# A two-layer attention and GLU kernel on one core: key copies and wo splits on GpSimd, weight squares and query products ahead of the first scores

## The chip, the cores and the metric

The kernel runs on one core of a Trainium2 chip. A core has a matrix engine (TensorE, PE in the profile, its weight loads PEld), a vector engine (VectorE, DVE), an activation engine (ScalarE, ACT), GpSimd (POOL) and an engine that mostly issues transfers (SyncE, SP). Each works through its own list of instructions in order. The metric is device time in microseconds, as the median of several runs.

## The reference

Two layers of the same weights; each is attention and a gated linear unit, both with a residual.

```python
def _A_ref(x, wq, wk, wv, wo):
    q = (x @ wq).reshape(B, S, H, Dh).transpose(0, 2, 1, 3)
    k = x @ wk
    v = x @ wv
    scores = jnp.einsum("bhqd,bkd->bhqk", q, k) * (Dh ** -0.5)
    p = _softmax(scores, axis=-1)
    o = jnp.einsum("bhqk,bkd->bhqd", p, v)
    return o.transpose(0, 2, 1, 3).reshape(B, S, H * Dh) @ wo

def _B_ref(x, w_gate, w_up, w_down):
    g = jnp.einsum("bsd,df->bsf", x, w_gate)
    u = jnp.einsum("bsd,df->bsf", x, w_up)
    return jnp.einsum("bsf,fd->bsd", _sigmoid(g) * u, w_down)

x = x + _A_ref(_layernorm(x), ...);  x = x + _B_ref(_layernorm(x), ...)   # twice
```

S is 2048, D 448, F 1792; 16 heads of 28 share one set of keys and values. The transposes are written shorter here than in the source.

## The kernel before

**Numbers.** Products of 32-bit values are made from 16-bit halves: each operand is split into a high part and a remainder, and one product is a chain of eleven matmuls (line 363). A weight is scaled by a power of two first, which is found from the sum of its squares: `squares` (L109) on ScalarE, `scales` on VectorE. `wo` is split on the way in by `split_d` (ScalarE the high part, VectorE the remainder, L130 and L131) and `split_p` (ScalarE, then GpSimd in two operations, L135 to L137), in turn.

**First stage.** The loop over `i` takes sixteen tiles of 128 rows of x through normalisation, the high/low split `hl` (remainder on GpSimd, L333 and L334), transposes (t, then XT on ScalarE, L348), the product with the key and value weights (kv), and `build()`: ScalarE writes the key's high part `ktl` and the value VV, VectorE the key's remainder (L394), and a copy (L396) repeats the high part six times. An iteration later `kvt` (L402, L403) transposes that into keys, and ScalarE copies them to KK (L406). Every four tiles GpSimd finds the group's reciprocal deviation in eight small operations (L317 to L325).

**Query products.** `qp` are chains at L363; ScalarE evicts each one to `qst` (L420) and, ahead of the main loop, to `qf` (L423) as well; GpSimd makes the remainder (L428), and a transfer that it issues (L435) stores both to `qd`, from which SP's queue loads QS.

**Maxima.** Before a query block's scores, each row's maximum over the keys has to be known. `Maxima.step()` makes four products `mx` (L556) and four reductions on VectorE (L561); a query block of 512 takes sixteen steps. After the last, `row_max` (L572) reduces, transposes (`mt`), copies (`mr`), and GpSimd issues the transfer of `mr` into QS (L585). `first_mx` calls the steps of query block 0 from the first stage: from iteration `SM` on one in each iteration, then the rest.

**Main loop.** A step is one query block u and one key tile kt. In the order `FSFSFSFSPXM` it issues fillers F (pieces of query products, later of the GLU), four score products s (L591) with an exponential on ScalarE each (P, L594), the previous step's pv (L602), and a maxima step of the next query block. The steps listed in `MORE` make two maxima steps. All but pv share seven banks of PSUM.

**Weights of the GLU.** `prep_b` is a generator: wo's load, its squares, its split, then 24 pieces (8 of each of three weights, 128x784, L194) whose squares are summed, then splits of columns and rows. `PLAN` gives how many of its steps have been taken by a step of the main loop, and `first_mx` takes some ahead of it. Pieces lie in the two buffers of tag XT2.

The lines that decide the order around the change:

```python
SM = L4 + 3 + 1
...
    if i >= SM:
        first_mx()
        nmx += 1
```

Of the kernel before, what the change touches and what calls it, by code (L numbers as in the profile page):

```python
# [8 lines left out]
F32 = mybir.dt.float32  # L9
# [10 lines left out]
def interleaved_layers_kernel(ctx: ExitStack, tc: tile.TileContext, x, wq, wk, wv, wo, wg, wu, wd, out, layers=2):  # L20
# [6 lines left out]
    nc = tc.nc  # L27
    _, S, D = x.shape
# [154 lines left out]

    def prep_b():

        NPG = 8
        mall = wk1.tile([128, 3, NPG], F32, name="mall", bufs=1)
        FL = D * F // 128 // NPG
        todo, raw = [], []

        def piece(w, i):
            wf = w.rearrange("a b -> (a b)").rearrange("(p n) -> p n", p=128)
            r = wk1.tile([128, FL], F32, tag="XT2", name="rmax")
            nc.sync.dma_start(r, wf[:, i * FL:(i + 1) * FL])  # L194
            return r

        def columns(f):
            r = big.tile([128, 2, 4, 128], F32, tag="big", name="rgu")
            for j, w in enumerate((wg, wu)):
                load4(r[:, j], w[:, f * 128:(f + 1) * 128])  # L200
            return r

        def rows(f):
            r = big.tile([128, 2, D], F32, tag="big", name="rd")
            nc.sync.dma_start(r, wd[f * 128:(f + 2) * 128].rearrange("(j p) n -> p j n", p=128))
            return r

        def get():

            while todo and len(raw) < 2:  # L210
                fn, *args = todo.pop(0)
                raw.append(fn(*args))
            return raw.pop(0)


        ro = [wk1.tile([128, 2, D], F32, tag="x1", name="ro") for _ in range(2)]
        for c in range(2):
            nc.gpsimd.memset(ro[c], 0.0)
            for g in range(G):
                nc.sync.dma_start(ro[c][32 * g:32 * g + Dh],  # L220
                                  wo[(4 * g + 2 * c) * Dh:(4 * g + 2 * c + 2) * Dh].rearrange("(h d) n -> d h n", d=Dh))
        yield
        parts = wk1.tile([128, 2], F32, name="parto", bufs=1)
        for c in range(2):
            junk = wk1.tile([128, 2, D], F32, tag="XT2", name="juno")
            squares(parts[:, c:c + 1], ro[c], junk)
        yield
        nc.vector.tensor_reduce(mxb[:, 0:1], parts, axis=AX.X, op=OP.add)
        yield
        yield from scales(mxb[:, 0:1], 1, pwb[:, 0:1], swb[:, 0:1])  # L230
        nc.vector.tensor_scalar(osc, pwb[:, 0:1], pwa[:, 1:2], 2.0 ** -23, op0=OP.mult, op1=OP.mult)
        for c in range(4):
            (split_d, split_p)[c % 2](WO[:, 0, c], WO[:, 1, c], ro[c // 2][:, c % 2], swb[:, 0:1])
            if c == 2:
                todo += [(piece, w, i) for w in (wg, wu, wd) for i in range(NPG)]
                for _ in range(2):
                    fn, *args = todo.pop(0)
                    raw.append(fn(*args))
            yield
        ready[0] = 1  # L240


        for n in range(3 * NPG):
            r = raw.pop(0) if raw else get()
            squares(mall[:, n // NPG, n % NPG:n % NPG + 1], r, r)
            while todo and len(raw) < 2:
                fn, *args = todo.pop(0)
                raw.append(fn(*args))
            yield
        todo += [(columns, f) for f in range(FC)] + [(rows, f) for f in range(0, FC, 2)]  # L250
        raw.append(columns(todo.pop(0)[1]))
        nc.vector.tensor_reduce(mxb[:, 1:4], mall, axis=AX.X, op=OP.add)
        yield
        yield from scales(mxb[:, 1:4], 3, pwb[:, 1:4], swb[:, 1:4])
        nc.vector.tensor_scalar(gsc, pwb[:, 1:2], 2.0 ** -26, None, op0=OP.mult)
        nc.vector.tensor_scalar(dsc, pwb[:, 2:3], pwb[:, 3:4], 2.0 ** -23, op0=OP.mult, op1=OP.mult)
        for f in range(FC):
            r = get()
            st = big.tile([128, 2, 2, 4, 128], F16, tag="big", name="sgu")
            for j in (1, 0):  # L260
                (split_d, split_pp)[j](st[:, j, 0], st[:, j, 1], r[:, j], swb[:, 1 + j:2 + j])
                if j == 0:
                    def store(f=f, st=st):
                        nc.gpsimd.dma_start(wgu_d[f].rearrange("p j l c n -> p (j l c n)"),
                                            st.rearrange("p j l c n -> p (j l c n)"))
                        ready[0] += 1
                    defer(store, 3)
                yield
        for f in range(0, FC, 2):
            r = get()  # L270
            for j in range(2):
                (split_d, split_pp)[1 - j](WD[:, f + j, 0], WD[:, f + j, 1], r[:, j], swb[:, 3:4])
            yield
        ready[0] += 1
        yield


    PLAN = [(0, 8), (28, 32), (31, 35), (63, 63), (71, 70)]
    prepd = [0]

    def paced(step):
# [100 lines left out]
    def kv(l, XT, t, kt, start=False):  # L382

        p = fps([128, 56], F32, "kv")
        yield from chain(p, lambda a, c, k: WKV[:k, a, c], lambda c, k: XT[:k, c, t * 128:(t + 1) * 128], 40, False)
        kt_ = ktl[kt % 2]

        def build():
            if start:
                nc.scalar.activation(kt_[:, 0, 0:28], p[:, 0:28], AF.Copy, scale=2.0 ** -18)  # L390
            else:
                nc.vector.tensor_scalar(kt_[:, 0, 0:28], p[:, 0:28], 2.0 ** -18, None, op0=OP.mult)
            nc.scalar.activation(VV[l][:, kt, 0:28], p[:, 28:56], AF.Copy, scale=2.0 ** -16)
            nc.vector.scalar_tensor_tensor(kt_[:, 1, 0:28], p[:, 0:28], 2.0 ** -18, kt_[:, 0, 0:28],  # L394
                                           op0=OP.mult, op1=OP.subtract)
            nc.vector.tensor_copy(kt_[:, 2:8, 0:28], kt_[:, 0:1, 0:28].to_broadcast([128, 6, 28]))  # L396
        defer(build)

    def kvt(l, kt, ev=nc.vector.tensor_copy):
# [563 lines left out]
    pkv, pq = prep_kv(), prep_q()  # L963
    nmx, nst, LEAD = 0, 0, 2
    SQ = L2 + 3 + 1
    SM = L4 + 3 + 1
    A0 = 0.5
    PRE, POST = {7: 2}, {6: 1, 8: 1, 9: 2, 10: 2}

    def first_mx():  # L970

        while QDONE.get((0, 0), 0) <= nmx % G and QDONE.get((0, 0), 0) < G:
            fill.slice(QCH / 2)
        if nmx == 0 or 3 < nmx < 12:
            next(prep[0])
            prepd[0] += 1
        mxs[0].step()

    for i in range(NT + L4):
# [30 lines left out]
    while nmx < 4 * NB:  # L1010
        fill.slice(A0E * QCH)
        first_mx()
        nmx += 1

    early[0] = False
    ORDER = "FSFSFSFSPXM"
    MORE = (5, 10)
    HEAD = (U * KT - 32, U * KT - 28, U * KT - 16)
    FIRST = KT * TB + 17
    KEEP = 28000  # L1020
# [1 line left out]
    for l in range(layers):  # L1022
# [3 lines left out]
            late.pop(0)[1]()  # L1026
        if not l:
            mx.step()
        if not final:
            layer_tiles(l + 1)  # L1030
        if l:
            for b in range(2, NB):
                fill.add(qgen(l, b), G * QCH)
        flush(True)
        fill.slice(0.75 * QCH)
        prevP = None
        rate = 0.0
        for step in range(U * KT):
# [91 lines left out]
```

## Time and profile before

| what | us |
|---|---|
| median of the runs (2326.1 to 2327.1) | 2326.68 |
| the profiled execution | 2324.3 |
| its span | 2321.3 |
| start of the first exponentials of the main loop | 93.69 |
| start of those of step 32 (query block 2) | 205.26 |
| start of those of step 52 | 277.33 |

The span is one execution's, from its first to its last instruction; some 3 us of the execution lie around it. A row of a timeline reads: start, duration, engine, line and operation, tile written and tile read, their shapes, how many stand in the row, and in brackets the idle time ahead of it with what ended it. A row of windows gives each engine's busy time in a stretch, then the clock granted to TensorE as a share of the full one, the share of the DMA engines' time, and GB/s.

### The profile page before, as it was taken

Reading aid. Unit: us, or ns where it says so; the run is one execution under the profiler, and the core shown is the slowest. Engines: PE = TensorE matmul, PEld = TensorE weight load, DVE = VectorE, ACT = ScalarE, POOL = GpSimd, SP = SyncE. Lnnn points to the kernel's source line nnn. Section 1 sums busy time; section 2 is a strip of 40 time slices with the busy share of each in tenths; the row PEclk is TensorE's granted clock in tenths of the full one; section 3 lists DMA queues with packets and bytes.
Section 4 is the critical chain, followed back from the end, with each engine's and each line's share of the span. In section 5 each row is a group of like instructions: output and inputs, shape, how many; then the busy total and the mean of one; then the engine's idle time right before and its main releaser. Section 6 shows DMA issues by size and latency. Waiting matters only on the chain.

```text
span 2321.3 us, 41368 instructions
## 1 busy us (share of the span) xinstructions
PE 2225.1 (96%) x15786; PEld 1004.9 (43%) x15786; DVE 1638.1 (71%) x2908; ACT 1585.8 (68%) x2614; POOL 339.4 (15%) x606
## 2 busy tenths in 40 slices
PE   5898899999999999999999999999999999999999
PEld 3222244444444444444563224444444444444456
DVE  6888887777777777777884557767677777767322
ACT  6698777677767777776515887767676767767731
POOL 6204762100110110101002010000000000000010
PEclk9799999999999999999999999999999999999999
DMA  4244671423313132332341113223231313223233
GB/s 118 68 118 126 203 223 41 107 76 95 101 61 108 44 110 73 95 98 76 106 132 40 30 54 100 78 83 98 72 87 57 107 47 105 68 83 95 76 101 114
DMA packets 205639, 213.28 MB, mean 92 GB/s; under 512 B 137520, under 2 KB 165872, under 8 KB 205440
## 3 DMA queue, kind: packets, MB, share of 16 engines
q1 hardware_dynamic: 200064, 195.77, 28.9%
q0 software_dynamic: 5376, 14.87, 1.9%
q8 instruction: 123, 2.02, 0.4%
q14 instruction: 76, 0.62, 0.1%
HBM read 175.37 MB, written 23.59 MB: 86 GB/s over the span
## 4 chain that ended last, share of the span: by engine, by line
PE 57%; DVE 3%; DMA 1%; ACT 1%; issue 1%; SPq 0%; POOL 0%; DVEq 0%; POOLq 0%; ACTq 0%
PE pv L602 13%; PE s L591 12%; PE dn L791 8%; PE up L363 8%; PE gp L363 8%; PE mx L556 4%; DVE mp L561 2%; PE wo L702 2%; PE qp L363 1%; ACT P L594 1%; DMA wgu<-wgu_d 1%; SPq L459 0%; DVE oT L683 0%; DVE th L761 0%; DMA XT<-hl 0%
## 5 line engine op out<-in xcount | busy, mean ns | idle before, releaser
L594 ACT ACTIVATE P<-s,esc 128x512 f32<-128x512 f32 x2048 | 1323.8, 689 | 460.4 <-PE s L591 434.0
L561 DVE TENSOR_REDUCE mp<-mx 128x1 f32<-128x512 f32 x2048 | 1269.8, 683 | 422.0 <-PE mx L556 419.7
L591 PE MATMUL s<-QS,KK 96*128 96x512 f16 x2048 | 767.6, 383 | 42.4 <-DVE mp L561 20.8
L363 PEld LDWEIGHTS <-wgu 128*128 128x128 f16 x4928 | 457.9, 97 | 239.0 <-issue 95.9
L602 PE MATMUL pv<-P,VV 128*32 128x512 f32 x4096 | 548.8, 608 | 0.0
L363 PE MATMUL gp<-XT,wgu 128*128 128x256 f16 x2464 | 375.0, 273 | 0.0
L363 PE MATMUL up<-XT,wgu 128*128 128x256 f16 x2464 | 373.9, 273 | 0.5 <-ACT P L594 0.4
L791 PE MATMUL dn<-WD,h 128*128 128x448 f16 x1344 | 321.0, 353 | 0.0
L591 PEld LDWEIGHTS <-KK 96*128 96x128 f16 x2048 | 197.5, 97 | 155.6 <-issue 60.4
L556 PE MATMUL mx<-KK,QH 32*128 32x512 f16 (+1 forms) x2080 | 222.3, 386 | 10.0 <-ACT P L594 4.0
L556 PEld LDWEIGHTS <-QH 32*128 32x128 f16 x2080 | 53.9, 91 | 393.1 <-issue 390.6
L791 PEld LDWEIGHTS <-h 128*128 128x128 f16 x1344 | 124.1, 98 | 137.7 <-issue 25.5
L602 PEld LDWEIGHTS pv<-P,VV 128*32 128x32 f32 x4096 | 81.1, 108 | 200.4 <-issue 198.0
L764 ACT ACTIVATE h<-th 128x512 f16<-128x512 f32 x112 | 70.3, 628 | 108.5 <-DVE th L761 108.3
L676 POOL TENSOR_TENSOR lb<-pvs,lb 128x512 f32<-128x512 f32 x32 | 40.9, 1278 | 608.3 <-DMA lb<-sums 517.1
L317 POOL TENSOR_SCALAR rs<-mv 128x1 f32<-128x1 f32 (+2 forms) x52 | 12.2, 234 | 797.1 <-DVE mv L302 757.1
L363 PE MATMUL qp<-XT,WQ 128*128 128x512 f16 x352 | 117.7, 400 | 1.9 <-DVE mp L561 0.7
L765 DVE SCALAR_TENSOR_TENSOR h<-th,h 128x512 f16<-128x512 f32 x112 | 78.9, 704 | 34.5 <-ACT h L764 34.5
L753 ACT ACTIVATE th<-gp,gsc 128x512 f32<-128x512 f32 x112 | 76.6, 684 | 38.5 <-PE gp L363 38.4
L761 DVE SCALAR_TENSOR_TENSOR th<-th,up 128x512 f32<-128x512 f32 x112 | 76.1, 680 | 37.3 <-PE up L363 30.9
L702 PE MATMUL wo<-WO,oT 128*128 128x448 f16 x384 | 94.7, 358 | 4.4 <-ACT oT L682 4.3
L363 PEld LDWEIGHTS <-WQ 128*128 128x128 f16 x352 | 34.1, 100 | 67.2 <-issue 43.5
(134 smaller groups left out, 847.2 us busy)
## 6 DMA issues: line engine op xcount, KB each, us to landing
wgu<-wgu_d SPq DMA_DIRECT2D x224, 512.0 KB
QS<-qd SPq DMA_DIRECT2D x384, 32.0 KB
lb<-sums SPq DMA_DIRECT2D x128, 64.0 KB
xr<-in_A_x_dram SPq DMA_DIRECT2D x32, 224.0 KB
qd<-qst POOLq DMA_DIRECT2D x28, 256.0 KB, 2.6
wgu_d<-sgu POOLq DMA_DIRECT2D x14, 512.0 KB, 3.8
QH<-qd SPq DMA_DIRECT2D x28, 128.0 KB
x2d<-x SPq DMA_DIRECT2D x16, 224.0 KB
```

The lines of the kernel that those rows point to most:

```text
L363: nc.tensor.matmul(ps, a, b, start=n == 0, stop=n == 10)
L556: nc.tensor.matmul(ps[h][:, i * w:(i + 1) * w], qh[32 * h:32 * h + 32, g], KK[l][32 * h:32 * h + 32, 1, ka:kz], start=True, stop=True, til ...
L561: nc.vector.tensor_reduce(o, ps[h].rearrange("p (g k) -> p g k", g=n), axis=AX.X, op=OP.max)
L591: nc.tensor.matmul(s, KK[l][0:96, 0, kt * 128:(kt + 1) * 128], QS[l, u][:, g].rearrange("p h n -> p (h n)"), start=True, stop=True)
L594: nc.scalar.activation(p, s, AF.Exp, scale=esc)
L602: nc.tensor.matmul(v[32 * g:32 * g + 32], VV[l][:, kt], P[g], start=kt == 0, stop=kt == KT - 1, tile_position=(0, 32 * g))
L702: nc.tensor.matmul(p, v["oT"][:, a, h * 128:(h + 1) * 128], WO[:, c, h], start=n == 0, stop=n == 11)
L753: defer(lambda: nc.scalar.activation(th, gp.rearrange("p j n -> p (j n)"), AF.Tanh, scale=gsc))
L761: nc.vector.scalar_tensor_tensor(t, th, 1.0, up.rearrange("p j n -> p (j n)"), op0=OP.add, op1=OP.mult)
L764: nc.scalar.activation(h[:, 0], t, AF.Copy, scale=2.0 ** -17)
L765: defer(lambda: nc.vector.scalar_tensor_tensor(h[:, 1], t, 2.0 ** -17, h[:, 0], op0=OP.mult, op1=OP.subtract), 1)
L791: nc.tensor.matmul(p, hs[f // 2][:, a, o:o + 128], WD[:, f, c], start=n == 0, stop=n == 3 * FC - 1)
```

## The change

GpSimd makes the copy of the key's parts in layer 0 from the fourth key tile on, and the remainder of all four parts of wo. The first maxima step comes an iteration earlier. The weights of the GLU are squared in 21 pieces of 128x896, whose buffers are three of tag `wgu` and two of XT2, so that up to five are on their way; 14 of the 21 come ahead of the first scores, with two evictions of query products between and behind them. Ten more query products and one more maxima step are issued ahead of the first scores, and step 5 of the main loop makes one maxima step instead of two.

```diff
-        NPG = 8
+        NPG = 7
...
-        def piece(w, i):
+        def piece(w, i, k):
...
-            r = wk1.tile([128, FL], F32, tag="XT2", name="rmax")
+            if k % 5 < 3:
+                r = wk1.tile([128, FL], F32, tag="wgu", name="rmax", bufs=WB)
+            else:
+                r = wk1.tile([128, FL], F32, tag="XT2", name="rmax")
...
-        def get():
-
-            while todo and len(raw) < 2:
+        def fetch(n):
+            while todo and len(raw) < n:
                 fn, *args = todo.pop(0)
                 raw.append(fn(*args))
+
+        def get():
+            fetch(2)
             return raw.pop(0)
...
+        todo += [(piece, w, i, NPG * j + i) for j, w in enumerate((wg, wu, wd)) for i in range(NPG)]
+        fetch(3)
         yield
...
         for c in range(4):
-            (split_d, split_p)[c % 2](WO[:, 0, c], WO[:, 1, c], ro[c // 2][:, c % 2], swb[:, 0:1])
...
+            split_p(WO[:, 0, c], WO[:, 1, c], ro[c // 2][:, c % 2], swb[:, 0:1])
+            fetch(5)
             yield
...
         for n in range(3 * NPG):
-            r = raw.pop(0) if raw else get()
+            r = get()
             squares(mall[:, n // NPG, n % NPG:n % NPG + 1], r, r)
...
+            fetch(4)
             yield
...
-    PLAN = [(0, 8), (28, 32), (31, 35), (63, 63), (71, 70)]
+    PLAN = [(0, 23), (24, 30), (31, 32), (63, 60), (71, 67)]
...
-            nc.vector.tensor_copy(kt_[:, 2:8, 0:28], kt_[:, 0:1, 0:28].to_broadcast([128, 6, 28]))
+            eng = nc.gpsimd if l == 0 and kt > 2 else nc.vector
+            eng.tensor_copy(kt_[:, 2:8, 0:28], kt_[:, 0:1, 0:28].to_broadcast([128, 6, 28]))
...
-    SM = L4 + 3 + 1
+    SM = L4 + 3
...
+    def advance(n):
+        for _ in range(n):
+            next(prep[0])
+            prepd[0] += 1
+
     def first_mx():
...
-        if nmx == 0 or 3 < nmx < 12:
-            next(prep[0])
-            prepd[0] += 1
+        advance(1 if nmx == 0 or 3 < nmx < 12 else 2 if nmx == 12 else 3 if nmx > 12 else 0)
         mxs[0].step()
...
+    advance(3)
+    fill.slice(1.2 * QCH)
     early[0] = False
     ORDER = "FSFSFSFSPXM"
-    MORE = (5, 10)
+    MORE = (10,)
...
         if not l:
             mx.step()
+            fill.slice(0.4 * QCH)
+            mx.step()
...
-        fill.slice(0.75 * QCH)
+        fill.slice((0.75 if l else 0.4) * QCH)
```

The engines' orders show where things came to stand. First GpSimd, before, in the first stage: `hl` is the remainder of x, `rs` the group's reciprocal deviation, `qst` the remainder of a query product.

```order
L333 TENSOR_TENSOR hl<-xr_153,hl 128x64
L334 TENSOR_TENSOR hl<-xr_153,hl 128x384
L317 TENSOR_SCALAR rs<-mv 128x4
L318 TENSOR_TENSOR rs<-rs,mhalf 128x4
L319 TENSOR_TENSOR rs<-rs 128x4
L320 TENSOR_TENSOR rs<-rs 128x4
L321 TENSOR_SCALAR rs<-rs 128x4
L322 TENSOR_TENSOR rs<-rs 128x4
L324 TENSOR_SCALAR rs<-mv 128x4
L325 TENSOR_TENSOR rs<-rs 128x4
L428 TENSOR_TENSOR qst<-qf,QH_125 128x512
L333 TENSOR_TENSOR hl<-xr_199,hl 128x64
```

The same place in the change:

```order
L398 COPY ktl_111<-ktl_111 128x6x28
L334 TENSOR_TENSOR hl<-xr_153,hl 128x64
L335 TENSOR_TENSOR hl<-xr_153,hl 128x384
L318 TENSOR_SCALAR rs<-mv 128x4
L319 TENSOR_TENSOR rs<-rs,mhalf 128x4
L320 TENSOR_TENSOR rs<-rs 128x4
L321 TENSOR_TENSOR rs<-rs 128x4
L322 TENSOR_SCALAR rs<-rs 128x4
L323 TENSOR_TENSOR rs<-rs 128x4
L325 TENSOR_SCALAR rs<-mv 128x4
L326 TENSOR_TENSOR rs<-rs 128x4
L430 TENSOR_TENSOR qst<-qf,QH_125 128x512
```

Here the next row is the copy of key tile 7, `L398 COPY ktl_112<-ktl_112 128x6x28`: it stands behind the eight operations of `rs` and the remainder of a query product; before, VectorE made it.

Second, GpSimd from the end of the first stage to the transfer of the maxima, before:

```order
L334 TENSOR_TENSOR hl<-xr_382,hl 128x384
L136 TENSOR_SCALAR ro<-ro,swb 128x448
L137 TENSOR_TENSOR WO<-ro,WO 128x448
L136 TENSOR_SCALAR ro<-ro,swb 128x448
L137 TENSOR_TENSOR WO<-ro,WO 128x448
L428 TENSOR_TENSOR qst<-qf,qst 128x512
L435 DMA qd_108<-qst 128x2x512
L585 DMA QS<-mr 1x16x128
```

And in the change, from the second of the four splits of wo on:

```order
L398 COPY ktl_111<-ktl_111 128x6x28
L136 TENSOR_SCALAR ro<-ro,swb 128x448
L137 TENSOR_TENSOR WO<-ro,WO 128x448
L398 COPY ktl_112<-ktl_112 128x6x28
L136 TENSOR_SCALAR ro<-ro,swb 128x448
L137 TENSOR_TENSOR WO<-ro,WO 128x448
L430 TENSOR_TENSOR qst<-qf,qst 128x512
L437 DMA qd_108<-qst 128x2x512
L430 TENSOR_TENSOR qst<-qf,qst 128x512
L437 DMA qd_108<-qst 128x2x512
```

The transfer of the maxima (`L587 DMA QS<-mr 1x16x128`) follows on the last row. Each of the last three copies stands behind a split of wo, and the maxima's transfer behind two remainders and two transfers to `qd` rather than one of each.

Third, ScalarE at the same place, before:

```order
L130 ACTIVATE WO<-ro,swb 128x448
L406 COPY KK<-kvt 128x2x128
L135 ACTIVATE WO<-ro,swb 128x448
L420 ACTIVATE qst<-qp 128x512
L423 ACTIVATE qf<-qp 128x512
L420 ACTIVATE qst<-qp 128x512
L594 ACTIVATE P<-s,esc 128x512 x8
L109 ACTIVATE rmax,mall<-rmax 128x784
```

And in the change:

```order
L135 ACTIVATE WO<-ro,swb 128x448
L408 COPY KK<-kvt 128x2x128
L109 ACTIVATE rmax,mall<-rmax 128x896 x8
L422 ACTIVATE qst<-qp 128x512
L425 ACTIVATE qf<-qp 128x512
L109 ACTIVATE rmax,mall<-rmax 128x896 x6
L422 ACTIVATE qst<-qp 128x512
L425 ACTIVATE qf<-qp 128x512
L422 ACTIVATE qst<-qp 128x512
L596 ACTIVATE P<-s,esc 128x512 x4
L109 ACTIVATE rmax,mall<-rmax 128x896
```

Squares (`rmax`, a piece) stand between the last keys and the two evictions, and in the main loop fewer stand between the exponentials.

More of the change, by code (lines that the diff above doesn't have):

```diff
@@ L232, in prep_b @@
         for c in range(4):
-            (split_d, split_p)[c % 2](WO[:, 0, c], WO[:, 1, c], ro[c // 2][:, c % 2], swb[:, 0:1])
[L234 to L238, printed above, removed]
+            split_p(WO[:, 0, c], WO[:, 1, c], ro[c // 2][:, c % 2], swb[:, 0:1])
+            fetch(5)
             yield
@@ L243, in prep_b @@
         for n in range(3 * NPG):
-            r = raw.pop(0) if raw else get()
+            r = get()
             squares(mall[:, n // NPG, n % NPG:n % NPG + 1], r, r)
-            while todo and len(raw) < 2:
-                fn, *args = todo.pop(0)
-                raw.append(fn(*args))
+            fetch(4)
             yield
```

## The prediction

> **What bounds the kernel now.** The page's busy times come first, because they say where a saved microsecond can count.
>
> ```profile
> PE 2225.1 (96%) x15786; PEld 1004.9 (43%) x15786; DVE 1638.1 (71%) x2908; ACT 1585.8 (68%) x2614; POOL 339.4 (15%) x606
> ```
>
> TensorE is busy for 96% of 2321.3 us. It waits mainly in the beginning, and from step 52 of the main loop on every engine's order is the same in both kernels. So the whole difference has to arise before step 52, and I read only that part: windows of ten microseconds around the last preparation, then the timeline.
>
> ```profile
> core 0: us, PE busy (x) PEld busy (x) DVE busy (x) ACT busy (x) POOL busy (x), PEclk, DMA share, GB/s
> 70.00:80.00 10.00, 8.72 (x40) 2.37 (x40) 10.00 (x21) 2.87 (x8) 4.89 (x4) 0.50 0.00 1
> 80.00:90.00 10.00, 5.75 (x28) 1.52 (x28) 9.24 (x18) 1.08 (x2) 2.30 (x3) 0.84 0.08 26
> 90.00:100.00 10.00, 9.78 (x41) 2.94 (x39) 7.14 (x14) 6.90 (x13) 1.00 (x2) 0.81 0.08 28
> ```
>
> Between 70 and 90 us VectorE is full, ScalarE nearly empty (3.95 of 20 us), and the DMAs carry almost nothing. That is the hole the change works in. The timeline shows what ends it:
>
> ```profile
> 76.33 12.04 DVE L561 TENSOR_REDUCE mp<-mx 128x1 f32<-128x512 f32 x20
> 81.07 0.60 ACT L420 ACTIVATE qst<-qp 128x512 f16<-128x512 f32 x1 [6.15 <-PE qp L363]
> 82.23 1.16 POOL L428 TENSOR_TENSOR qst<-qf,qst 128x512 f16<-128x512 f32 x1 [4.69 <-ACT qf L423]
> 83.69 0.84 POOL L435 DMA_DIRECT2D qd<-qst  x1 [0.30 <-POOL qst L428]
> ...
> 89.64 3.60 PE L363 MATMUL qp<-XT,WQ 128*128 128x512 f16 x8
> 89.70 0.54 POOL L585 DMA_DIRECT2D QS<-mr  x1 [5.17 <-DVE mr L584]
> ...
> 93.02 1.46 PE L591 MATMUL s<-QS,KK 96*128 96x512 f16 x4
> ...
> 93.69 4.73 ACT L594 ACTIVATE P<-s,esc 128x512 f32<-128x512 f32 x8 [1.54 <-PE s L591]
> ```
>
> VectorE's reductions end at 88.4; the maxima are put into QS by a transfer that GpSimd issues at 89.70; the scores stand behind it, and the first exponentials start at 93.69. Call that moment the start of the loop.
>
> Inside the loop two things set a step:
>
> ```profile
> 98.29 0.88 ACT L109 ACTIVATE rmax<-rmax 128x784 f32<-128x784 f32 x1
> ...
> 102.24 2.48 ACT L594 ACTIVATE P<-s,esc 128x512 f32<-128x512 f32 x4
> ...
> 105.36 0.77 ACT L594 ACTIVATE P<-s,esc 128x512 f32<-128x512 f32 x1
> ...
> 108.95 2.54 ACT L594 ACTIVATE P<-s,esc 128x512 f32<-128x512 f32 x4
> ...
> 113.52 2.56 ACT L594 ACTIVATE P<-s,esc 128x512 f32<-128x512 f32 x4 [1.19 <-PE s L591]
> ...
> 118.28 2.42 ACT L594 ACTIVATE P<-s,esc 128x512 f32<-128x512 f32 x4 [2.21 <-PE s L591]
> ```
>
> A step with one square takes 3.12 us (102.24 to 105.36), one with a square and an eviction of query products 3.59 (105.36 to 108.95), and ScalarE is full in both. The two steps around the doubled maxima of step 5 take 9.33 (108.95 to 118.28). A step without a square isn't shorter by the square:
>
> ```profile
> 162.59 5.00 ACT L594 ACTIVATE P<-s,esc 128x512 f32<-128x512 f32 x8
> ...
> 164.43 0.39 PE L556 MATMUL mx<-KK,QH 32*128 32x512 f16 x4
> ...
> 164.85 2.48 DVE L561 TENSOR_REDUCE mp<-mx 128x1 f32<-128x512 f32 x4 [0.68 <-PE mx L556]
> ...
> 166.50 1.07 PE L602 MATMUL pv<-P,VV 128*32 128x512 f32 x8
> ...
> 167.49 0.40 PE L556 MATMUL mx<-KK,QH 32*128 32x512 f16 x4
> ```
>
> This is step 20, in which ScalarE runs from one step's exponentials into the next one's (eight in a row) with no square between. From one set of maxima products to the next it takes 3.06 us (164.43 to 167.49): the products wait for banks of PSUM that the reductions free, the last score waits for the second reduction, pv (1.07) follows, then the next products. VectorE idles 0.68 in it. So a square removed from a plain step brings 0.06 us, not its 0.9.
>
> **The change part by part.** *Key parts on GpSimd, first maxima an iteration earlier.* GpSimd's copy now stands in the middle of its queue:
>
> ```profile
> 46.55 0.23 POOL L317 TENSOR_SCALAR rs<-mv 128x4 f32<-128x4 f32 x1
> ...
> 48.48 0.23 PE L402 MATMUL kvt<-id,ktl 128*128 128x128 f16 x1
> ...
> 49.44 0.20 POOL L325 TENSOR_TENSOR rs<-rs 128x4 f32<-128x4 f32 x1
> 49.59 1.15 POOL L428 TENSOR_TENSOR qst<-qf,QH 128x512 f16<-128x512 f32 x1
> ...
> 50.97 0.91 POOL L334 TENSOR_TENSOR hl<-xr,hl 128x384 f16<-128x384 f32 x1
> ```
>
> Before, key tile 7 was transposed at 48.48, in the middle of GpSimd's eight small operations for a group's rstd (46.55 to 49.64). Now its copy stands behind these and behind a query remainder (1.15). The stretch ahead of them grows, too, by one maxima step and six query products; six at 0.45 (3.60 for eight) are 2.7, some of it beside other work, so I take 2.0. Then: rstd from 48.5 to 51.6, remainder to 52.8, copy to 53.3, so +4.8. The copy has no row on GpSimd. Below it lies VectorE's own time for a smaller group, above it 0.91 for 384 elements of two inputs; I take 0.5, since the 0.23 for four elements and 168 parts of 384 of the rest make 0.53.
>
> The Trainium skill (GPSIMD Engine Reference, 4.1 Engine selection) has elementwise work with two inputs about twice as slow on GpSimd as on VectorE, and with one input at roughly line rate. No row of before shows a copy on GpSimd; at VectorE's rate the loop's start would come about 1 us earlier than I say, by an estimate from that page.
>
> What waits for the late copy is the transpose, then ScalarE's KK, then the maxima, and behind KK on ScalarE all of the next tiles. The tiles up to KK at 65.04 follow at their old pace, and then come the tiles that share GpSimd with wo:
>
> ```profile
> 65.04 0.36 ACT L406 COPY KK<-kvt 128x256 f16<-128x256 f16 x1
> ...
> 70.83 1.41 POOL L136 TENSOR_SCALAR ro<-ro,swb 128x448 f32<-128x448 f32 x1 [4.45 <-ACT WO L135]
> ...
> 72.33 1.03 POOL L137 TENSOR_TENSOR WO<-ro,WO 128x448 f16<-128x448 f32 x1
> ...
> 73.98 0.37 ACT L406 COPY KK<-kvt 128x256 f16<-128x256 f16 x1 [1.42 <-PE kvt L403]
> ```
>
> One split of wo takes GpSimd 2.53 (70.83 to 73.36), and in the new order each of three copies stands behind one: 3.03 with the copy, some 3.45 with the hand-over to ScalarE and back. Three make 10.35 where 8.94 passed (65.04 to 73.98), so +1.4; hidden, it is 0, with a whole hand-over in series +2.8. The last KK ends at 74.35 + 6.2 = 80.55. VectorE loses two splits and thirteen copies, which I count as nothing, since it is not last any more: its row maximum comes at about 91, and if it did bound, these would be worth 2 to 4 us.
>
> *Fourteen squares ahead.* ScalarE does eight, evicts a query product, does six, evicts another.
>
> ```profile
> 55.33 0.95 ACT L109 ACTIVATE juno<-ro 128x896 f32<-128x896 f32 x1
> ...
> 61.00:62.00 1.00, 0.90 (x15) 0.78 (x15) 1.00 (x3) 0.91 (x3) 0.09 (x1) 0.50 1.00 386
> ```
>
> Fourteen at 0.95 (the same width, 896) are 13.3; two evictions for both halves, 1.16 each (81.07 to 82.23), 2.3. Pieces of 459 KB at 386 GB/s take 1.2 each: five are fetched ahead and nine are 10.7, less than the squares, but a buffer is refilled only when its square is done. I add 1.0 (0 to 2.3). ScalarE is through at 97.15. Now the order matters: GpSimd's issue of QS<-mr stands behind the remainder and the qd transfer of that second eviction: 1.16, 0.30 and 0.84 later is 99.45, where 89.70 was. From issue to exponentials took 3.99, partly behind the eight products that ended at 93.24; with these done earlier I take 3.6. **The loop starts at 103.0, 9.3 later.** If no copy waits and the feed is free it is 2.1; with every upper bound 12. Ten more query products and four maxima products ahead lie in TensorE's idle time (4.25 us in 80 to 90) and are counted as nothing; uncovered, the ten are 4.5. Transfers of pieces on SP's queue stand ahead of QS loads of the next query block, sixteen steps away.
>
> *What the loop gets back.* Of the four plain steps with a square and an eviction (3.59) one is left: 3 x 0.53 = 1.6. A dozen other squares at 0.06: 0.7. One of two doubled maxima: 9.33 - 6.12 = 3.2 here; the other one, which stays, may get it instead, so 2.5. And a stall late in the block:
>
> ```profile
> 178.62 0.86 ACT L109 ACTIVATE rmax<-rmax 128x784 f32<-128x784 f32 x1 [1.05 <-DMA rmax<-in_B_w_down_dram]
> 179.47 2.40 ACT L594 ACTIVATE P<-s,esc 128x512 f32<-128x512 f32 x4
> ...
> 185.55 2.48 DVE L561 TENSOR_REDUCE mp<-mx 128x1 f32<-128x512 f32 x4 [2.65 <-PE mx L556]
> ...
> 187.96 2.42 ACT L594 ACTIVATE P<-s,esc 128x512 f32<-128x512 f32 x4 [1.36 <-PE s L591]
> ```
>
> A square waits 1.05 for its piece, the exponentials behind it are late, and two steps take 8.49 (179.47 to 187.96) where 6.12 would do. The squares are gone from there: 2.4 + 1.05 = 3.4 (0 if something else holds the steps). Sum: 8.2.
>
> *The clock.* TensorE was granted 0.50 up to 80 us, and 0.84 and 0.81 in the next two windows. It now idles some 5 us ahead of the first scores, so I expect the first step or two at half rate: +2.0 (0 to 3).
>
> The Trainium skill (TensorE: Matmul & The Clock Gate, Part 1: The HAM clock gate) says that an idle window of about 3.4 us halves the clock and about 3.4 us of busy time restore it. By it a step bound by TensorE would lose about 1.7 us, an estimate from that page; the 0.81 above agrees with such a stretch.
>
> **Sum:** 9.3 - 8.2 + 2.0 = +3.1 us. The profiled execution took 2324.3 (its span is 2321.3) and would take 2327.4; the median of the runs shown is 2.4 above it. So 2326.7 + 3.1 = **2329.8 us**. What this kernel's measurement can tell from no change is about 0.2%, 4.65 us: 2322.0 to 2331.3 counts as the same.
>
> **The rivals.**
>
> *The loop follows its engines' sums (2320.2).* If the chain of 3.06 is only as long as ScalarE's squares let the phases drift, a bare step costs the larger of 2.48 on VectorE, 2.3 on ScalarE and some 2.65 on TensorE: 0.4 less in 24 steps, 9.6 more. For it: VectorE idles 0.68 in step 20. Against it: ScalarE had no square in that step, and 3.06 remained.
>
> *The copies don't wait (2322.6).* If ScalarE, not GpSimd, paces the tiles, the last KK stays at 74.35 and the feed is free: 7.2 less. For it: GpSimd idles 4.45 ahead of 70.83. Against it: the order puts copies behind three splits, and a queue can't be overtaken.
>
> *The stall at steps 24 to 27 stays (2333.2, slower).* If it isn't the square but the bank of a late reduction that holds TensorE there, 3.4 less is repaid. For it: the second wait, 2.65, is VectorE's for TensorE's products, with no DMA in it. Against it: that wait follows the late exponentials. It decides from 1.5 us of stall on, since 2329.8 is that far from the bound.
>
> **Chances.** The forecast 0.36 (of it 0.22 the same, 0.13 slower, 0.01 faster by the bounds of its terms); engines' sums 0.27 (0.25 faster, 0.02 the same); copies that don't wait 0.10 (0.04 faster, 0.06 the same); the stall that stays 0.27 (0.25 slower, 0.02 the same). So faster 0.30, the same 0.32, slower 0.38. The forecast's own range is 2325 to 2335. The whole range goes from 2316 (engines' sums with 4 us of the start's bounds) to 2338 (the stall that stays, with 5 us of them).
>
> **What would show it.** In the changed profile: kvt of key tile 7 near 53.3; last KK near 80; fourteen squares end near 97 with VectorE done near 91; QS<-mr issued by GpSimd directly behind a qd transfer near 99.5; first exponentials near 103; bare steps of 3.06; no wait in steps 24 to 27; a granted clock of 0.5 in the first step or two. It is wrong if the exponentials start before 97 us, if bare steps take under 2.8, or if the two kernels still drift apart behind step 52.

## The result, and the profile after

| | before | after |
|---|---|---|
| median of twelve runs each | 2326.39 | 2326.67 |
| ratio, 95% interval | | 1.0003 [0.9995, 1.0011] |
| span of the profiled execution | 2321.3 | 2324.2 |
| start of the last KK copy of the first stage | 74.0 | 81.7 |
| end of the row maximum's first reduction | 88.6 | 93.7 |
| issue of the transfer of the maxima | 89.7 | 102.3 |
| first exponentials (step 0) | 93.7 | 106.9 |
| step 32 | 205.3 | 212.6 |
| step 52 | 277.3 | 283.9 |

No difference can be measured: the interval reaches from 1.2 us less to 2.6 us more. Inside, much has moved. The loop starts 13.3 us later, the first 32 steps take 105.6 us instead of 111.6, and 6.5 us of loss are left at step 52, 2.9 at the end. These are single executions: against a second profile of the kernel before, the loss is 4.8 at step 52 and 4.1 at the end.

The windows of the changed kernel, with the columns of those shown before (busy us of PE, PEld, DVE, ACT, POOL, granted clock, DMA share, GB/s):

```profile
70.00:80.00 10.00, 7.35 (x66) 3.93 (x65) 7.58 (x16) 6.58 (x17) 8.02 (x10) 0.50 0.00 0
80.00:90.00 10.00, 7.93 (x31) 2.16 (x32) 9.29 (x16) 7.29 (x16) 3.65 (x4) 0.61 0.58 193
90.00:100.00 10.00, 7.84 (x25) 2.40 (x25) 4.79 (x11) 8.97 (x18) 2.02 (x2) 0.66 0.97 343
100.00:110.00 10.00, 5.64 (x20) 1.55 (x18) 5.71 (x13) 3.65 (x7) 3.18 (x4) 0.74 0.51 190
```

ScalarE's hole is filled (7.29 and 8.97 instead of 1.08 and 6.90), and VectorE, which was full, now has holes itself (4.79 and 5.71). The timeline of the same kernel names them, in the order of the chain:

```profile
53.77 0.32 POOL L398 COPY ktl<-ktl 128x168 f16<-128x168 f16 x1
...
59.83 0.35 ACT L408 COPY KK<-kvt 128x256 f16<-128x256 f16 x1
...
81.72 0.37 ACT L408 COPY KK<-kvt 128x256 f16<-128x256 f16 x1 [1.55 <-PE kvt L405]
...
88.69 0.95 ACT L109 ACTIVATE rmax<-rmax 128x896 f32<-128x896 f32 x1 [0.85 <-DMA rmax<-in_B_w_gate_dram]
...
92.16 0.58 PE L558 MATMUL mx<-KK,QH 32*128 32x512 f16 x1 [2.48 <-ACT qf L425]
92.19 1.16 POOL L430 TENSOR_TENSOR qst<-qf,qst 128x512 f16<-128x512 f32 x1 [8.46 <-ACT qf L425]
92.67 5.58 PE L364 MATMUL qp<-XT,WQ 128*128 128x512 f16 x13
...
98.18 0.22 PE L584 MATMUL mt<-id,m 128*16 128x128 f16 x1
...
100.09 1.14 POOL L430 TENSOR_TENSOR qst<-qf,qst 128x512 f16<-128x512 f32 x1 [5.59 <-ACT qf L425]
101.53 0.75 POOL L437 DMA_DIRECT2D qd<-qst  x1 [0.30 <-DMA rmax<-in_B_w_down_dram]
102.27 0.54 POOL L587 DMA_DIRECT2D QS<-mr  x1
...
106.31 1.89 PE L593 MATMUL s<-QS,KK 96*128 96x512 f16 x4 [4.05 <-DMA QS<-mr]
```

Key tile 7's copy starts at 53.77 on GpSimd. The last maxima product waits 2.48 us for an eviction that stands behind eight squares; the transposition of the maxima (mt, 98.18) stands behind thirteen query matmuls, and the transfer (102.27) behind the second remainder and its transfer to qd. Then TensorE waits 4.05 us for that transfer alone: it landed 4.0 us behind its issue, where in the kernel before it took 1.7 and the scores stood behind query matmuls instead.

A plain step of the loop in the changed kernel:

```profile
153.83 2.42 ACT L596 ACTIVATE P<-s,esc 128x512 f32<-128x512 f32 x4 [0.17 <-PE s L593]
156.35 2.48 DVE L563 TENSOR_REDUCE mp<-mx 128x1 f32<-128x512 f32 x4 [0.58 <-PE mx L558]
156.90 2.42 ACT L596 ACTIVATE P<-s,esc 128x512 f32<-128x512 f32 x4 [0.65 <-PE s L593]
```

It takes 3.07 us (153.83 to 156.90) with both engines idle for a part of it; the shortest step of the first 32 took 2.80.

### The profile page after: what moved, and what is told of

Its sections match the earlier page's. It is cut to its first block, busy times and chain, and to the rows that moved or that the text cites. A ratio compares the mean times of both kernels' runs of the same rounds, so it can differ in the third digit from the quotient of the medians.

```text
span 2324.2 us, 41358 instructions
## 1 busy us (share of the span) xinstructions
PE 2220.9 (96%) x15786; PEld 1004.1 (43%) x15786; DVE 1632.0 (70%) x2892; ACT 1588.1 (68%) x2609; POOL 348.4 (15%) x624
## 4 chain that ended last, share of the span: by engine, by line
PE 57%; DVE 4%; DMA 2%; ACT 1%; issue 1%; POOL 0%; SPq 0%; DVEq 0%; POOLq 0%; ACTq 0%
PE pv L604 13%; PE s L593 12%; PE dn L793 8%; PE up L364 8%; PE gp L364 8%; PE mx L558 4%; DVE mp L563 3%; PE wo L704 2%; PE qp L364 1%; ACT P L596 1%; DMA wgu<-wgu_d 1%; DMA QS<-mr 0%; DVE oT L685 0%; DVE th L763 0%; DMA XT<-hl 0%
## 5 line engine op out<-in xcount | busy, mean ns | idle before, releaser
L558 PE MATMUL mx<-KK,QH 32*128 32x512 f16 (+1 forms) x2080 | 217.2, 387 | 10.0 <-ACT P L596 3.6
```

What stands on the lines that cost most here:

```text
L558: nc.tensor.matmul(ps[h][:, i * w:(i + 1) * w], qh[32 * h:32 * h + 32, g], KK[l][32 * h:32 * h + 32, 1, ka:kz], start=True, stop=True, til ...
```

## The experiments

Each kernel's profile gives the times along the chain; each is one execution. "Issue" is that of the maxima's transfer, s0, s32 and s52 the first exponentials of these steps. The ratio is to the runs of the kernel before on the same chip.

| kernel | last KK | issue | s0 | s32 | s32 - s0 | s52 | span | ratio [95%] |
|---|---|---|---|---|---|---|---|---|
| before | 74.0 | 89.7 | 93.7 | 205.3 | 111.6 | 277.3 | 2321.3 | |
| before again | 73.6 | 89.3 | 93.3 | 204.8 | 111.5 | 279.1 | 2320.1 | one run |
| the change | 81.7 | 102.3 | 106.9 | 212.6 | 105.6 | 283.9 | 2324.2 | 1.0003 [0.9995, 1.0011] |
| copies on VectorE | 75.1 | 95.4 | 99.4 | 208.3 | 108.9 | 280.9 | 2322.3 | 0.9982 [0.9973, 0.9991] |
| maxima's transfer first | 81.3 | 93.7 | 102.2 | 207.1 | 104.9 | 278.6 | 2319.4 | 0.9990 [0.9981, 0.9999] |
| squares in the loop | 81.0 | 94.4 | 97.2 | 205.0 | 107.8 | 275.3 | 2316.3 | 0.9963 [0.9951, 0.9975] |
| three mended | 74.2 | 86.7 | 93.9 | 199.4 | 105.6 | 271.9 | 2311.5 | 0.9960 [0.9948, 0.9972] |
| before, only copies moved | 76.5 | 91.4 | 94.8 | 207.9 | 113.1 | 278.7 | 2321.1 | 0.9996 [0.9987, 1.0005] |
| mended, wo in turn | 74.9 | 87.7 | 96.0 | 203.0 | 107.0 | 272.6 | 2315.5 | 0.9971 [0.9962, 0.9981] |
| before, only deeper feed | 73.2 | 89.0 | 92.9 | 201.1 | 108.1 | 275.2 | 2316.0 | 0.9967 [0.9956, 0.9977] |
| mended, shorter fill | 74.7 | 87.1 | 92.8 | 197.1 | 104.4 | 271.5 | 2314.5 | 0.9954 [0.9940, 0.9968] |
| mended, old maxima | 74.6 | 87.0 | 91.0 | 199.6 | 108.6 | 269.8 | 2311.6 | 0.9947 [0.9933, 0.9962] |
| mended, squares ahead | 75.0 | 87.7 | 95.6 | 201.6 | 106.0 | 271.4 | 2313.6 | 0.9956 [0.9940, 0.9971] |

**The kernel before again**, unchanged.

> The kernel before, unchanged, to learn how much two executions of it differ behind step 52, where both kernels have the same order. Theory A (the loss of 6.5 us that the changed kernel shows at step 52 is its own, and the 3.6 us that it wins back later are chance): start of the first exponentials 93.7 within 0.5, step 52 at 277.3 within 1, and from step 52 to the end 2047 or so, 1 to 5 us more than the 2044.0 of the first profile. Theory B (the later gain belongs to the change): step 52 to the end 2044.0 within 0.5.

From step 52 to the end it took 2041.1 us, where the first profile took 2044.0 and the changed kernel 2040.4. Neither theory's number came: the direction that I expected was wrong, and step 52 came 1.8 later, not within 1. But the point stands: of the 3.6 us that the change seems to win back behind step 52, 2.9 lie in the first profile of the kernel before. Two executions of one kernel also differ by 2.2 us between steps 32 and 52. The traces show where, at the first scores of step 48 (query block 3), in this execution and in the first one:

```profile
263.27 0.39 PE L591 MATMUL s<-QS,KK 96*128 96x512 f16 x1 [2.90 <-DMA QS<-mr]
262.13 0.39 PE L591 MATMUL s<-QS,KK 96*128 96x512 f16 x1 [1.65 <-DMA QS<-mr]
```

The maxima's transfer was waited for 1.25 us longer, and from 263.9 to 267.2 the granted clock was 0.50 here and 1.00 there, so that step 48 took 5.44 instead of 4.31. So the profiles tell parts of the beginning to within half a microsecond where the granted clock is the same, and whole spans only to some three.

**Copies on VectorE.**

```diff
-            eng = nc.gpsimd if l == 0 and kt > 2 else nc.vector
-            eng.tensor_copy(kt_[:, 2:8, 0:28], kt_[:, 0:1, 0:28].to_broadcast([128, 6, 28]))
+            nc.vector.tensor_copy(kt_[:, 2:8, 0:28], kt_[:, 0:1, 0:28].to_broadcast([128, 6, 28]))
```

> The changed kernel with the key parts' copies back on VectorE. Theory A (GpSimd's queue delays the keys, and ScalarE's squares stand behind the last keys): last KK copy at 77 to 78 instead of 81.7, first exponentials at 102 to 103.5 instead of 106.95, step 52 near 280 instead of 283.9. Rival (the feed of the pieces sets the end of the squares): last KK earlier by the same, but the squares wait for pieces by as much more, first exponentials within 1 us of 106.95. Second rival (the copies weigh on VectorE): last KK earlier, the end of the row maximum not.

The last KK came 6.6 us earlier, more than expected, the row maximum with it (86.4 instead of 93.7), and the loop started 7.6 earlier. The copies, and not VectorE's load, held the keys. The transfer of the maxima is still waited for:

```profile
95.39 0.54 POOL L586 DMA_DIRECT2D QS<-mr  x1
...
98.72 1.89 PE L592 MATMUL s<-QS,KK 96*128 96x512 f16 x4 [4.97 <-DMA QS<-mr]
...
139.26 1.94 PE L603 MATMUL pv<-P,VV 128*32 128x512 f32 x8
```

Only 3.0 of the 7.6 us are left at step 52: steps 0 to 32 took 3.3 us more than in the changed kernel, most of it in step 1 (4.01 instead of 3.11) and step 11 (5.19 instead of 3.23). Both lie where the granted clock was 0.50: 100 to 105 us, and 136.8 to 143.5, where the eight pv took 1.94 (last row) instead of 1.07. In the changed kernel, with the same order in the loop, the clock was 1.00 in step 11. By its runs this kernel is 0.18% under the kernel before.

**The maxima's transfer first.**

```diff
+    while late:
+        late.pop(0)[1]()
     advance(3)
     fill.slice(1.2 * QCH)
```

> The changed kernel with the transposition of the maxima and their transfer into QS ahead of the last three squares' group and of the 13 query matmuls that stood ahead of them; on GpSimd the transfer then stands ahead of the second query remainder. Theory A (the loop starts late because that transfer stands behind the second remainder): the transfer issued near 95 instead of 102.27, first exponentials near 100.2, behind ScalarE's last square and evictions, so 6.7 earlier; step 52 near 277.2; time 0.25 to 0.3% less than the changed kernel's. Rival (the transfer is slow because the pieces fill the DMA engines): issued at 95, landing only when the pieces are through, first exponentials at 103 or later.

The transfer was issued at 93.7, 8.6 us earlier, but the loop started only 4.8 us earlier. The timeline of this kernel shows what came in its place:

```profile
93.09 4.67 PE L364 MATMUL qp<-XT,WQ 128*128 128x512 f16 x13
...
98.26 0.95 ACT L109 ACTIVATE rmax<-rmax 128x896 f32<-128x896 f32 x1 [1.59 <-DMA rmax<-in_B_w_up_dram]
...
100.33 0.39 PE L558 MATMUL mx<-KK,QH 32*128 32x512 f16 x3 [0.95 <-ACT qf L425]
...
101.74 0.81 PE L593 MATMUL s<-QS,KK 96*128 96x512 f16 x3
```

The last square waits 1.59 us for its piece, the eviction behind it is late, three maxima products of the next block wait for that eviction's bank, and the scores stand behind these. The rival's slow transfer is there as well: it landed 6.1 us behind its issue, near 99.8, but the scores could not have started before 101.74 anyway. The time fell by half of what I expected (0.9990 against 1.0003).

**Squares in the loop.**

```diff
-        advance(1 if nmx == 0 or 3 < nmx < 12 else 2 if nmx == 12 else 3 if nmx > 12 else 0)
+        advance(1 if nmx == 0 or 3 < nmx < 12 else 0)
...
-    advance(3)
...
-    PLAN = [(0, 23), (24, 30), (31, 32), (63, 60), (71, 67)]
+    PLAN = [(0, 8), (28, 29), (31, 32), (63, 60), (71, 67)]
```

> The changed kernel with only the first of its three groups of steps ahead of the loop (the wo part), and all 21 squares in the loop, as before. Theory A: row maximum near 90, first exponentials near 96 to 97 (10 us earlier than 106.95), last KK still near 81.7; the stretch from step 0 to step 32 109 to 110 us instead of 105.6; step 52 near 278. If the squares ahead cost nothing net (rival: what they delay the loop gets back in full), step 52 stays near 283.9.

The loop started 9.7 us earlier, and the 21 squares in it cost only 2.2 us more from step 0 to 32 (107.8). This kernel is 0.37% faster than before. Its transfer of the maxima, which landed 2.1 us behind its issue, is not waited for at all:

```profile
94.43 0.54 POOL L587 DMA_DIRECT2D QS<-mr  x1
...
95.70 1.25 PE L364 MATMUL qp<-XT,WQ 128*128 128x512 f16 x5
...
96.79 0.78 PE L593 MATMUL s<-QS,KK 96*128 96x512 f16 x2
```

From issue to scores 2.36 us passed, with query matmuls between, where the change needed 4.04.

**The three mended**: the three edits together.

> The three edits of the runs so far together: copies on VectorE, the maxima's transfer first, all 21 squares in the loop. Theory A (copies, position of the transfer and squares each delay the same chain, keys to maxima to transfer to scores): last KK near 75, row maximum near 86, transfer issued near 88.5, first exponentials 91.5 to 93; the stretch from step 0 to step 32 107.8 as with the squares in the loop alone; step 52 near 270.5; time 0.5 to 0.65% under the kernel before's. Rival (once the chain is short, the evictions or TensorE's fillers bind): first exponentials at 95 or later, time 0.4% under.

The keys and the transfer came as expected or somewhat earlier, the loop started at 93.9, between theory and rival, and the time is the rival's (0.40% under). The transfer landed 3.3 us behind its issue, near 90; behind the maxima's transposition TensorE's queue was the last:

```profile
86.07 4.28 PE L364 MATMUL qp<-XT,WQ 128*128 128x512 f16 x13
86.18 0.21 DVE L585 COPY mr<-mt 16x128 f16<-16x128 f16 x1 [0.37 <-PE mt L583]
86.69 0.55 POOL L586 DMA_DIRECT2D QS<-mr  x1 [2.86 <-DVE mr L585]
...
92.36 1.25 PE L364 MATMUL qp<-XT,WQ 128*128 128x512 f16 x5
...
93.45 0.78 PE L592 MATMUL s<-QS,KK 96*128 96x512 f16 x2
```

The scores come 6.76 us behind the issue, directly behind the last query matmuls. Steps 0 to 32 took 105.6, as in the changed kernel, although all 21 squares lie in them.

**Before, only the copies moved** to GpSimd.

```diff
-            nc.vector.tensor_copy(kt_[:, 2:8, 0:28], kt_[:, 0:1, 0:28].to_broadcast([128, 6, 28]))
+            eng = nc.gpsimd if l == 0 and kt > 2 else nc.vector
+            eng.tensor_copy(kt_[:, 2:8, 0:28], kt_[:, 0:1, 0:28].to_broadcast([128, 6, 28]))
```

> The kernel before with the key parts' copies on GpSimd and nothing else. Theory A (the copies alone delay the keys, since they stand behind rstd's eight operations and the splits): last KK 4 to 7 us later (78 to 81), first exponentials 4 to 6 later (97.5 to 99.5), step 52 later by as much, time 0.15 to 0.25% over before. Rival (it is the four splits of wo in the same queue): last KK at most 2 later.

My theory was too large: 2.5 us at the last KK and 1.1 at the start, and no difference in time. By its timeline the delay comes at the one place named, behind the group's reciprocal deviation (`rs`) and a query remainder, and hardly grows:

```profile
49.57 0.20 POOL L325 TENSOR_TENSOR rs<-rs 128x4 f32<-128x4 f32 x1
49.72 1.15 POOL L429 TENSOR_TENSOR qst<-qf,QH 128x512 f16<-128x512 f32 x1
50.82 0.33 POOL L397 COPY ktl<-ktl 128x168 f16<-128x168 f16 x1
...
73.24 1.42 POOL L136 TENSOR_SCALAR ro<-ro,swb 128x448 f32<-128x448 f32 x1 [1.68 <-ACT WO L135]
```

So the 7.7 us of the change at the last KK need both: without its copies it loses 1.1, with the copies alone 2.5. Which of the other edits in that stretch (four splits of wo, the earlier maxima, the six query matmuls) leaves the copies no room was not tested one by one.

The steps of this kernel differ from the kernel before by the granted clock. Steps 5 and 6, with the doubled maxima in both, took 7.8 us here at 1.00, and 9.3 there, where it was 0.50 from 114.4 to 117.7 and the eight pv in it took 1.93 instead of 1.07. Steps 24 to 27 took 20.0 instead of 16.9, with 0.50 in two stretches (182.8 to 186.1 and 189.6 to 192.9).

**Mended, wo in turn**: the three mended, with the two splits back on VectorE.

```diff
-            split_p(WO[:, 0, c], WO[:, 1, c], ro[c // 2][:, c % 2], swb[:, 0:1])
+            (split_d, split_p)[c % 2](WO[:, 0, c], WO[:, 1, c], ro[c // 2][:, c % 2], swb[:, 0:1])
```

> The three mended, and wo split in turn on VectorE and GpSimd as before. Theory A (with the copies gone from GpSimd the four splits there are hidden, and two splits on VectorE cost it 1.4 us in the stretch that its reductions fill): row maximum up to 1.4 later, first exponentials 0 to 1.4 later than with the three mended. Rival (GpSimd's splits delay the last query remainder and the transfer behind it): first exponentials 1 to 2 earlier.

The row maximum came 1.0 later and the loop started 2.2 later, more than the 1.4 of the two splits; the rival's gain didn't come. Step 11 took 4.7 instead of 3.2, again at a granted clock of 0.50 (133.1 to 136.4). The intervals of the two ratios overlap.

**Before, only the deeper feed**: 21 pieces of 896 with five buffers and the change's `fetch`, all squared in the loop; the rest as before.

> The kernel before with the weights' pieces alone changed: 21 pieces of 128x896 with five buffers, all squared in the loop. Theory A (the stall at steps 24 to 27 is a late piece, and a deeper feed ends it without moving any square): first exponentials 93.3 to 93.7 as before, steps 24 to 27 together 13.6 instead of 16.9, step 52 3 to 4 us earlier, time 0.1 to 0.2% under before. Theory B, the prediction's (only squares moved away end it) and the rival that a bank of a reduction holds it: steps 24 to 27 stay above 16.

The start was that of before (92.9), steps 24 to 27 took 13.0 us instead of 16.9, and the kernel is 0.33% faster, more than expected. Its exponentials in the place of the stall:

```profile
177.93 2.45 ACT L595 ACTIVATE P<-s,esc 128x512 f32<-128x512 f32 x4
...
181.14 2.48 ACT L595 ACTIVATE P<-s,esc 128x512 f32<-128x512 f32 x4
183.42 1.03 ACT L109 ACTIVATE rmax<-rmax 128x896 f32<-128x896 f32 x1
...
184.86 4.83 ACT L595 ACTIVATE P<-s,esc 128x512 f32<-128x512 f32 x8
```

No row waits, squares stand between, and two steps take 6.93 (177.93 to 184.86) instead of 8.49. The 21 squares reach to 189.6, so none had to leave these steps. The edit makes the pieces larger and starts the first ones earlier as well; which of these, beside the five buffers, ended the wait was not separated.

**Mended, shorter fill.**

```diff
-    fill.slice(1.2 * QCH)
+    fill.slice(0.4 * QCH)
```

> The three mended with 0.4 instead of 1.2 of a query chunk behind the maxima's transfer, so 71 query matmuls ahead of the first scores instead of 80. Theory A (the first scores, whose maxima have landed near 89.6, wait behind the query matmuls on TensorE until 93.45): first exponentials 90.5 to 91.5, 2.5 to 3.4 earlier; the nine matmuls cost the loop nothing, since TensorE doesn't bind its steps: step 0 to 32 105.5 to 106, step 52 near 269; time 0.1 to 0.15% under that of the three mended. Rival (the prediction's: query products ahead are free, because they lie in idle time, and behind step 0 they cost 0.4 each): first exponentials within 1 us of 93.9, step 52 the same or up to 3.6 later.

The start came 1.1 us earlier, less than half of what I expected, since the maxima products and the later query matmuls still stand ahead of the scores at 92.35, while the transfer had landed near 88.8. Step 52 came 0.4 earlier. Its time can't be told from that of the three mended.

**Mended, old maxima.**

```diff
-    MORE = (10,)
+    MORE = (5, 10)
...
             mx.step()
-            fill.slice(0.4 * QCH)
-            mx.step()
...
-        fill.slice((0.75 if l else 0.4) * QCH)
+        fill.slice(0.75 * QCH)
```

The 1.2 of a chunk ahead are left out as well.

> The three mended with the maxima of query block 1 as before: one step ahead of the loop, steps 5 and 10 doubled, and 66 query matmuls ahead of the first scores. Theory A (the second maxima step ahead of the loop saves about 2 us in steps 5 and 6 and delays the start by what its products and fillers take): first exponentials 90 to 91, steps 5 and 6 together 9.3 to 9.7 instead of 6.9, steps 10 and 11 7.8 instead of 8.7, step 0 to 32 107 to 108 instead of 105.5; step 52 within 1.5 of the shorter fill's. Rival (the doubled step is free, its stall is only made up elsewhere): step 0 to 32 the same as with one.

The loop started at 91.0, 2.8 us earlier, and steps 0 to 32 took 3.0 us more: steps 5 and 6 took 10.2 instead of 6.9 (with a granted clock of 0.50 from 112.4 to 115.7), steps 10 and 11 8.7 in both. By this run the second maxima step ahead costs at the start what it saves in the loop; but 14 query matmuls less stand ahead as well, so the 2.8 are not its alone. At 2314.71 us this is the fastest median that was run, 0.53% under before; the intervals of four mended kernels overlap, and even that of the deeper feed alone reaches into this one.

**Mended, squares ahead**: the change with only copies and transfer mended.

> The changed kernel with the copies on VectorE and the maxima's transfer first, its 14 squares ahead of the first scores kept: beside the three mended it differs by the squares' place alone. Theory A (squares ahead delay the last maxima through the eviction that stands behind eight of them, and bring the loop 0.1 us each or less): row maximum near 86.4 as with the copies on VectorE alone, transfer issued 87 to 88, first exponentials at 95 to 97, behind ScalarE's last squares; step 0 to 32 1 to 2.5 us shorter than with the three mended; net 0 to 2 us slower at step 52. Rival (the squares ahead are free once the transfer no longer stands behind them): first exponentials within 1 us of 93.9 and step 52 1 to 2 earlier.

The start is 1.7 us later than with the squares in the loop, steps 0 to 32 are not shorter (106.0 and 105.6; step 11 took 4.1 instead of 3.2, with a granted clock of 0.50 from 131.5 to 134.8), and the time is the same. The transfer landed 6.8 us behind its issue while the pieces moved, 0.7 ahead of the scores. Ahead or in the loop, the place of the fourteen squares makes no difference that could be measured once the rest of the chain is free.

Beside the kernel with the transfer first, this one differs by the copies alone: the start is 6.6 us earlier, step 52 7.2, and the ratio is 0.9956 instead of 0.9990, with intervals that don't touch.

## Why the prediction was right

No difference can be told, the median of 2326.67 lies in the range of 2325 to 2335, and the way there was the forecast one, a later start against shorter steps. The 3.1 us themselves did not come: the runs show 0.3, and 3.1 lies outside their interval, which ends at 2.6. Luck has a share in it. "The same" had been given 0.32 and "slower" 0.38; and in the profile the net loss at step 32, which was to be 3.1, is 7.3 (212.6 against 205.3).

**The start** was to be 9.3 us later and was 13.3, the largest miss of the sum. The places that I named were right, several sizes were not.

- Last KK, 81.7 instead of 80.2. What stands ahead of `rs` grew by 3.1 us (it starts at 49.65 instead of 46.55) and not by 2.0, the copy took 0.32 and not 0.5, and key tile 9's KK came 5.2 later (62.37 against 57.21) where I had 4.8. Key tile 8's is later by more (59.83 against 52.77), but only because the two squares of wo now stand ahead of it; before, they stood ahead of tile 9's. The tiles behind did not keep their old pace: key tile 12's KK follows in 3.73 instead of 2.74, with a split of wo on ScalarE (71.01) and a wait for transposes (0.42) ahead of it. The three tiles between splits took 10.1, as forecast 10.35.
- The squares took 18.0 with their evictions instead of 16.6: three waits for pieces of 0.85, 0.37 and 0.57, where I had added 1.0.
- GpSimd's rows up to the issue took 2.3, as forecast.
- From the issue to the exponentials 4.68 instead of 3.6 passed. I had taken the 3.6 from the kernel before, where the transfer landed in 1.7 and query matmuls filled the rest; here it took 4.0 to land, and nothing else was waited for.

**VectorE's row maximum** was forecast near 91 and came at 93.7: I had seen that an eviction stands behind eight squares, and not that the last maxima product waits for its bank. The query products that I counted as nothing held the transposition of the maxima from 93.9 to 98.2. In the change neither shows, since GpSimd's second remainder ended later still (101.2); in the three mended, query products are the last thing that the scores wait for.

**What the loop gets back** was 8.2 less 2.0 for the clock, 6.2 net; measured are 5.9, by other shares. Squares moved out of the loop were to bring 2.3. With the transfer first, squares ahead and in the loop give 104.9 and 105.6 (other kernel 106.0): at most 0.6, less than two such kernels scatter. The doubled maxima were to bring 2.5 and bring 3.0 by the old maxima's run. But the 9.33 that I took for their cost holds a stretch at half clock: with the same doubled maxima at 1.00 the two steps took 7.8, so about half of the 3.2 that I read off was the clock. The stall of 3.4 went, but the step "the squares are gone from there" failed: with only the feed changed it went too, squares and all. A late piece behind a two-deep feed held ScalarE, not a square too many. The clock was to cost 2.0 and cost about 0.7, by the changed kernel's 12.7 us from step 0 to 4 (granted 0.50 from 105 to 110) against 12.0 with the transfer first (1.00), whose order in the loop is the same; that the clock is all that differs there is not shown.

**The rivals.** Bare steps took 3.07, and the loop won back 5.9 in all, where that rival wanted 9.6 more than the forecast: the loop doesn't follow its engines' sums. The copies wait, and without them the kernel is 0.18% under before. The stall doesn't stay. As for drift behind step 52, which was to prove me wrong: there is 3.6 us of it, and 2.9 are between two executions of the kernel before.

**What stays open.** By profiles the change loses 2.9 or 4.1 us, by medians 0.3 with 2.6 as its upper bound. Part of that scatter goes with the clock: of 25 runs of the kernel before, the 17 with a mean granted clock of 0.986 took 2325.9 us on average, the two with 0.989 2322.7. Single executions scatter too much to say more. Of the 7.4 us by which the deeper feed lowers the median, its profile shows 3.8 in steps 24 to 27; where the rest lies is not known.

The change thus holds one gain that the runs show, the deeper feed with its 0.33%, and what moved work into idle time gave it back: the copies, and the squares with the transfer of the maxima behind them, each lengthened the only chain that mattered there.

## What to carry to other kernels

An idle engine is free only where none of its results is waited for: before work is put into its idle time, look for the next instruction behind it in its queue and who waits for that; here it was an eviction behind eight squares. When several edits move together, test each alone and each left out: one that looked harmless alone cost 1.1 us at the start, and in company 7.6. Before a step's length is put down to what stands in it, read the clock granted in it: here two equal pairs of steps took 7.8 and 9.3 us. And when a wait disappears, ask which of the edits took it away, since here it was the deeper feed and not the moved work.

## What the runs showed of the hardware

A transfer of 4 KB (16x128 f16, QS<-mr) landed 1.6 to 1.7 us behind its issue in six of these kernels (the kernel before: DMA share 0.01 from 89 to 92). While weight pieces were moving it took 3.3, 4.0, 6.1 and 6.8 (6.1 with a DMA share of 1.02 from 93 to 100, 6.8 with 1.00 from 87 to 95). In two kernels it took 3.3 and 2.9 at a share of 0.02, for which I have no cause.

The granted clock was 0.50 in the step behind the doubled maxima of step 5 in four of the five profiles that double it (from 114.4 to 117.7 in the kernel before), and in the one behind step 10 in three of thirteen, though TensorE's longest gap there was 0.41 us. Eight pv took 1.93 or 1.94 us where all of them fell into such a stretch, beside 1.07 at 1.00, and the step took up to 2.0 us longer (5.19 instead of 3.23).

On GpSimd the copy of 168 16-bit elements per partition took 0.32 us, beside 0.19 to 0.20 in the shortest rows of the same on VectorE (up to 1.03 in others).
